# A two-layer decode step on one core: joint maximum before the second exponent, values in rows of (d, j), and the last wo in wide products

## The chip, the core and the metric

The kernel runs on one core of one Trainium2 chip. The time is device microseconds of one execution of the whole program, the median of several runs. The engines are TensorE (PE in the profile; PEld is its weight load), VectorE (DVE), ScalarE (ACT), GpSimd (POOL) and SyncE (SP), which here only issues transfers. SBUF is the on-chip memory of 128 partitions, PSUM the memory into which TensorE writes, in eight banks of 512 fp32 per partition.

## What is computed

Two attention layers and two feed-forward layers alternate, for a batch of 4 and one new token each, all in fp32. Both attention layers read the same caches and weights, both feed-forwards the same weights.

```python
def _A_ref(x, k_cache, v_cache, wq, wo):      # caches: (B=4, Hkv=8, Sk=4096, Dh=128); Hq = 32
    q = (x @ wq).reshape(B, Sq, Hq, Dh).transpose(0, 2, 1, 3)
    k, v = jnp.repeat(k_cache, 4, axis=1), jnp.repeat(v_cache, 4, axis=1)
    p = _softmax(jnp.einsum("bhqd,bhkd->bhqk", q, k) * Dh ** -0.5)
    o = jnp.einsum("bhqk,bhkd->bhqd", p, v)
    return o.transpose(0, 2, 1, 3).reshape(B, Sq, Hq * Dh) @ wo
def _B_ref(x, w1, w3, w2):                    # D = 512, F = 1792
    return (_silu(x @ w1) * (x @ w3)) @ w2
x = A_x
for _ in range(2):
    x = x + _A_ref(_layernorm(x), A_k_cache, A_v_cache, A_wq, A_wo)
    x = x + _B_ref(_layernorm(x), B_w1, B_w3, B_w2)
```

## The kernel before

**Data.** The host lays caches and weights out as one array of rows, 128 partitions wide, in the order in which they are used. SBUF holds one large buffer `space` of 218 slots of 1 KB per partition. The table LOADS lists the transfers in order: (first slot in the source, number of slots, place in `space`). `pump` issues the next transfer on SyncE's queue as soon as its place is free, and `done` frees a place behind the last product that reads it. Some rows stay in SBUF for the second layer, so 296.8 MB come from HBM in all.

**Attention.** A group is one key head with its four query heads. Layer 0 takes the groups 0 to 7, layer 1 the groups 7 to 0. The 4096 keys of a group come in two halves, `first` and `last`. TensorE, VectorE and ScalarE work in the order of the code; nothing reorders it:

- `score` multiplies q with eight tiles of keys into the bank `scores` (128 x 512: rows are batch, block of keys j and head; the columns are 512 keys). `between` puts other products behind a given tile: the turning of the group before (`turn_o`, tile 3), its wo product (`gather_o`, tile 5).
- `maximum` takes each row's negated maximum over its own half, `exponent` the exponential and its row sum, `turn` transposes p on TensorE and copies it out as pT, `weigh` multiplies pT with the values into the bank o_ps[0] or o_ps[1].
- `join_maxima` finds the maximum of each head over all its rows, by a 32 x 32 transpose on VectorE (`across`), and two factors that bring the rows of either half to it; `join_sums` joins the sums and takes the reciprocal.
- `finish` scales both banks into `both`, masks out the blocks that don't belong to the row, and adds the four blocks j up into `o`. The last group of a layer does it with one accumulation on VectorE for each block instead, so that those of o_ps[0] run beside the second `weigh`.
- q is made for two groups at a time: `share_q` leaves partial products in four bands of the bank `wide`, `take_q` evicts and scales them, `turn_q` adds the bands and transposes, `copy_q` places the result.
- wo: `gather_o` makes 4 wide products (8 x 512), whose four bands `take_o` evicts and `spread_o` adds up. The last group's `project_o` makes 16 products of 128 columns that need no such sum. A product in fp32 shows as two in the profile.

`busy` issues products of a unit matrix that nobody reads. `layernorm`, `feed_forward` and `down` follow, and in layer 0 `turn_over` leads to the next layer.

Of the kernel before, what the change touches and what calls it, by code (L numbers as in the profile page):

```python
# [8 lines left out]
F32 = mybir.dt.float32  # L9
# [6 lines left out]
REP = HQ // HKV  # L16
# [65 lines left out]
def tile_decode_layers(ctx: ExitStack, tc: tile.TileContext, rows, out):  # L82
# [116 lines left out]
    nc.vector.tensor_scalar(block, block, 2.0, None, op0=ALU.mult)  # L199
    nc.vector.tensor_copy(block[:, NB:], block[:, 0:NB])  # L200
# [37 lines left out]


# [99 lines left out]
    def spread_out():  # L339
        rows = across(rstd[:, 0:1])[:, 0:B]  # L340
        nc.vector.scalar_tensor_tensor(rows, rows, 1.0, alike, op0=ALU.mult, op1=ALU.mult, accum_out=spread)
# [43 lines left out]
    def exponent(i, ps, acc, scale=None):  # L385
        p = work.tile([P, NT, P], F32, name="p", bufs=1)
        nc.scalar.activation(p.rearrange("p n s -> p (n s)"), ps, AF.Exp, bias=acc[:, i:i + 1],  # L387
                             scale=1.0 if scale is None else scale, accum_out=acc[:, 2 + i:3 + i])
        return p
# [15 lines left out]
    def join_maxima(acc):  # L405
        nc.vector.tensor_tensor(acc[:, 6:7], acc[:, 0:1], acc[:, 1:2], op=ALU.min)
        rows = across(acc[:, 6:7])
        rows3 = rows.rearrange("p (j r) -> p j r", r=REP)
        nc.vector.tensor_tensor(rows3, rows3, other.unsqueeze(1).to_broadcast([P, 2 * NB, REP]), op=ALU.add)
        nc.vector.tensor_reduce(acc[:, 7:8], rows, axis=AX.X, op=ALU.min)  # L410
        nc.scalar.activation(acc[:, 4:6], acc[:, 0:2], AF.Exp, bias=acc[:, 7:8], scale=-1.0)

    def join_sums(acc, at_end):
        nc.vector.tensor_tensor(acc[:, 8:10], acc[:, 2:4], acc[:, 4:6], op=ALU.mult)
        nc.vector.tensor_tensor(acc[:, 10:11], acc[:, 8:9], acc[:, 9:10], op=ALU.add)
        rows = across(acc[:, 10:11])
        rows3 = rows.rearrange("p (j r) -> p j r", r=REP)
        nc.vector.scalar_tensor_tensor(rows3, rows3, 1.0, alike.unsqueeze(1).to_broadcast([P, 2 * NB, REP]),
                                       op0=ALU.mult, op1=ALU.mult, accum_out=acc[:, 11:12])
        nc.vector.reciprocal(acc[:, 11:12], acc[:, 11:12])  # L420
        if at_end:
            nc.vector.scalar_tensor_tensor(acc[:, 16:24].rearrange("p (i j) -> p i j", i=2),
                                           block.rearrange("p (i j) -> p i j", i=2), acc[:, 11:12],
                                           acc[:, 4:6].unsqueeze(2).to_broadcast([P, 2, NB]),
                                           op0=ALU.mult, op1=ALU.mult)
        else:
            nc.vector.tensor_scalar(acc[:, 16:16 + NB], block[:, 0:NB], acc[:, 11:12], None, op0=ALU.mult)
# [19 lines left out]
    def finish(layer, g, c, p, acc, at_end):  # L447
# [3 lines left out]
        join_sums(acc, at_end)  # L451
        if not at_end:
            both = work.tile([P, NB * DH], F32, name="both", tag="p", bufs=1)
            nc.scalar.activation(both, o_ps[0], AF.Copy, scale=acc[:, 4:5])  # L454
            weigh(layer, g, c, 1, pT)
            nc.vector.scalar_tensor_tensor(both, o_ps[1], acc[:, 5:6], both, op0=ALU.mult, op1=ALU.add)  # L456
            blocks = both.rearrange("p (j d) -> p j d", j=NB)
            nc.vector.tensor_tensor(blocks, blocks, acc[:, 16:16 + NB].unsqueeze(2).to_broadcast([P, NB, DH]), op=ALU.mult)  # L458
            o = work.tile([P, DH], F32, name="o", tag="pT", bufs=1)
            nc.vector.tensor_reduce(o, both.rearrange("p (j d) -> p d j", j=NB), axis=AX.X, op=ALU.add)  # L460
            return o
        o = work.tile([P, DH], F32, name="o", tag="p", bufs=1)
        nc.vector.tensor_scalar(o, o_ps[0][:, 0:DH], acc[:, 16:17], None, op0=ALU.mult)

        def add(s, js):
            for j in js:
                nc.vector.scalar_tensor_tensor(o, o_ps[s][:, j * DH:(j + 1) * DH],  # L467
# [17 lines left out]
    def project_o(layer, g):  # L485
        w = wo_of(g)
        for h in range(REP):
            for k in range(KC):
# [3 lines left out]
        nc.vector.scalar_tensor_tensor(x_sb, x_ps, 1.0, x_sb, op0=ALU.mult, op1=ALU.add,  # L492
                                       accum_out=rowsum)
# [125 lines left out]
    for layer in range(LAYERS):  # L619
# [5 lines left out]
        else:  # L625
# [5 lines left out]
            turn_q(take_q(spread), len(gs))  # L631
# [4 lines left out]
        for n, (g, (first, last)) in enumerate(order):  # L636
# [12 lines left out]
            pT = turn(p, nc.scalar.copy)  # L649
            between = {}  # L650
            if n in shared:
                shares = take_q(spread if len(gs) > 1 else rstd[:, 0:1])
# [12 lines left out]
            if layer and n == 0:  # L665
                spread_out()
# [11 lines left out]
        busy(BUSY[1])  # L678
        project_o(layer, g)
        busy(BUSY[2])  # L680
# [51 lines left out]
```

## Time and profile before

| | |
|---|---|
| median of 3 runs | 705.98 us (704.12 to 706.36) |
| the profiled execution | 702.22 us, its span 700.4 us |
| busy: PE, PEld, DVE, ACT, POOL | 408.4, 125.7, 128.1, 58.6, 3.4 us |
| moved | 297.35 MB, 425 GB/s on the mean |
| mean granted TensorE clock | 0.803 of full speed |
| chain of waits | DMA 68%, PE 26%, DVE 2% of the span |

The profile's page is of one execution. "Busy" is time in which an engine works on an instruction; the slices cut the span into 40 equal parts of 17.5 us. In a group's line stand the code's line, the engine, the operation, output and input by the program's names, their shapes, the count, the busy time with the mean of one in ns, and the idle time before them with what ended it. In a timeline a row is the start, the length, the engine and the instructions merged in it, in brackets the idle time of the engine ahead.

### The profile page before, as it was taken

To read this page: it belongs to the slowest core of one execution; us is meant where nothing else is said; L and a number is where in the kernel's file an instruction comes from. 1 tells how busy PE (TensorE), PEld (TensorE's weight loads), DVE (VectorE), ACT (ScalarE), POOL (GpSimd) and SP (SyncE) were. 2 spreads that over 40 slices of the span, in tenths; PEclk is the share of its full clock that TensorE was granted. 3 is DMA by queue.
4 is the path that set the end of the run, shared out by engine and by line. 5 is a ranking of instruction groups with operands and counts; after the bars stand their busy time and mean duration, and the time that the engine had idled before them with its cause. 6 is when DMAs were issued, how large, how long until landed. Compare 5 with 4: busy or idle time off the path is not lost.

```text
span 700.4 us, 7226 instructions
## 1 busy us (share of the span) xinstructions
PE 408.4 (58%) x3164; PEld 125.7 (18%) x3164; DVE 128.1 (18%) x394; ACT 58.6 (8%) x136; POOL 3.4 (0%) x15
## 2 busy tenths in 40 slices
PE   1245576545664519667686895544554626655677
PEld 0011121111211103121233331111111101111123
DVE  3012002120110103221221332011101201111322
ACT  0010000100100001010111300000100101001100
POOL 0000000000000000000000000000000000000000
PEclk9677668766788669877799998677968958688989
DMA  9999999999999999999999999999999999999997
GB/s 408 434 416 423 454 438 417 430 438 443 419 421 442 437 424 424 432 429 434 414 420 373 423 433 440 447 427 418 436 443 426 439 418 448 430 428 419 429 420 286
DMA packets 12704, 297.35 MB, mean 425 GB/s; under 512 B 1408, under 2 KB 1536, under 8 KB 4480
## 3 DMA queue, kind: packets, MB, share of 16 engines
q1 hardware_dynamic: 12672, 296.88, 99.1%
q8 instruction: 25, 0.41, 0.2%
q14 instruction: 7, 0.06, 0.0%
HBM read 296.81 MB, written 0.07 MB: 424 GB/s over the span
## 4 chain that ended last, share of the span: by engine, by line
DMA 68%; PE 26%; DVE 2%; another core or an unknown queue 1%; issue 1%; ACT 0%; SPq 0%; DVEq 0%; ACTq 0%
DMA space<-in_rows 68%; PE o L436 15%; PE scores L369 6%; PE turned L394 1%; PE o L525 1%; PE sums_ps L350 1%; DVE pT L396 1%; PE stored L290 1%; PE stored L571 0%; DVE o L467 0%; PE sums_ps L334 0%; PE sums_ps L489 0%; SPq L153 0%; PE sums_ps L579 0%
## 5 line engine op out<-in xcount | busy, mean ns | idle before, releaser
L369 PE MATMUL scores<-space,qT 128*32 128x512 f32 x1024 | 167.2, 737 | 135.0 <-DMA space<-in_rows 134.3
L436 PE MATMUL o<-space,pT 128*16 128x512 f32 x1024 | 148.4, 705 | 106.0 <-DMA space<-in_rows 97.5
L369 PEld LDWEIGHTS scores<-space,qT 128*32 128x32 f32 x1024 | 36.3, 126 | 215.3 <-issue 180.0
L436 PEld LDWEIGHTS o<-space,pT 128*16 128x16 f32 x1024 | 32.7, 108 | 202.7 <-issue 160.4
L381 DVE TENSOR_REDUCE acc<-scores 128x1 f32<-128x512 f32 x32 | 22.1, 691 | 183.7 <-PE scores L369 183.7
L387 ACT ACTIVATE p<-scores,acc 128x512 f32<-128x512 f32 x30 | 20.6, 687 | 412.9 <-DVE acc L381 305.1
L394 PE MATMUL turned<-ident,p 128*128 128x128 f32 x128 | 23.3, 310 | 16.6 <-ACT p L387 16.6
L396 DVE COPY pT<-turned 128x256 f32<-128x256 f32 x16 | 6.8, 424 | 141.2 <-PE turned L394 141.2
L394 PEld LDWEIGHTS turned<-ident,p 128*128 128x128 f32 x128 | 14.9, 152 | 49.2 <-ACT p L387 31.7
L456 DVE SCALAR_TENSOR_TENSOR both<-o,acc,both 128x512 f32<-128x512 f32 x14 | 10.5, 750 | 56.5 <-PE o L436 56.5
L454 ACT ACTIVATE both<-o,acc 128x512 f32<-128x512 f32 x14 | 9.6, 687 | 119.0 <-PE turned L394 119.0
L479 DVE COPY oT<-sums_ps 128x16 f32<-128x16 f32 x16 | 2.8, 175 | 86.2 <-PE sums_ps L478 86.2
L334 PE MATMUL sums_ps<-space,xT 128*32 128x512 f32 x120 | 16.7, 680 | 2.8 <-DMA space<-in_rows 2.8
L525 PE MATMUL o<-space,xT 128*32 128x192 f32 (+1 forms) x256 | 13.9, 355 | 3.8 <-DMA space<-in_rows 1.9
L460 DVE TENSOR_REDUCE o<-both 128x128 f32<-128x512 f32 x14 | 14.4, 1028 | 0.5
L499 PE MATMUL stored<-space,oT 128*8 128x512 f32 x104 | 13.6, 595 | 0.0
L478 PE MATMUL sums_ps<-columns,o 128*128 128x16 f32 x32 | 7.6, 315 | 5.4 <-DVE o L460 4.1
L478 PEld LDWEIGHTS sums_ps<-columns,o 128*128 128x128 f32 x32 | 6.0, 234 | 25.7 <-issue 13.3
L350 PEld LDWEIGHTS sums_ps<-same,shares 128*128 128x128 f32 x64 | 8.6, 209 | 10.1 <-DVE shares L345 5.1
L248 PE MATMUL o<-columns,same 128*32 128x1 f32 x64 | 2.0, 181 | 14.5 <-DVE columns L626 13.5
L350 PE MATMUL sums_ps<-same,shares 128*128 128x8 f32 (+1 forms) x64 | 9.3, 272 | 0.9 <-DVE shares L345 0.9
L458 DVE TENSOR_TENSOR both<-both,acc 128x512 f32<-128x512 f32 x14 | 9.7, 692 | 0.5
(119 smaller groups left out, 166.1 us busy)
## 6 DMA issues: line engine op xcount, KB each, us to landing
space<-in_rows SPq DMA_DIRECT2D x7, 4096.0 KB, 24.8
space<-in_rows SPq DMA_DIRECT2D x3, 6144.0 KB, 31.9
space<-in_rows SPq DMA_DIRECT2D x8, 2048.0 KB, 25.7
space<-in_rows SPq DMA_DIRECT2D x2, 7168.0 KB, 43.1
space<-in_rows SPq DMA_DIRECT2D x4, 3072.0 KB, 26.4
space<-in_rows SPq DMA_DIRECT2D x11, 1024.0 KB, 13.1
space<-in_rows SPq DMA_DIRECT2D x3, 3584.0 KB, 17.1
space<-in_rows SPq DMA_DIRECT2D x2, 5120.0 KB, 22.8
```

The lines of the kernel that those rows point to most:

```text
L334: nc.tensor.matmul(wide[32 * k:32 * k + 32, :], window(k, j), w[:, k, :], start=(j == 0), stop=(j == len(gs) - 1))
L350: nc.tensor.matmul(misc[:, h * n * B:(h + 1) * n * B], shares[:, h * DH:(h + 1) * DH], same[:, 0:n * B], start=True, stop=True)
L369: nc.tensor.matmul(ps[32 * b:32 * b + 32, :], qT[:, at:at + 32], u, start=(m < 2), stop=(m >= TILES - 2))
L381: nc.vector.tensor_reduce(acc[:, i:i + 1], ps, axis=AX.X, op=ALU.max, negate=True)
L387: nc.scalar.activation(p.rearrange("p n s -> p (n s)"), ps, AF.Exp, bias=acc[:, i:i + 1], scale=1.0 if scale is None else scale, accum_out ...
L394: nc.tensor.transpose(pt[:, n, :], p[:, n, :], ident)
L396: copy(pT, pt.rearrange("p n (b r) -> p n b r", b=B)[:, :, :, 0:ROW])
L436: nc.tensor.matmul(o_ps[i][32 * b:32 * b + ROW, :], pT[:, r // 2, b, :], t[:, j * NB * DH:(j + 1) * NB * DH], start=(r < 2), stop=(r >= TI ...
L460: nc.vector.tensor_reduce(o, both.rearrange("p (j d) -> p d j", j=NB), axis=AX.X, op=ALU.add)
L478: nc.tensor.matmul(at, o, head, start=True, stop=True)
L499: nc.tensor.matmul(bank[32 * h:32 * h + WIDE, :], oT[:, h, :], w[:, h, :], start=first, stop=last)
L525: nc.tensor.matmul(bank[32 * j:32 * j + 32, s], window(k), w[:, j], start=(k == 0), stop=(k == KC - 1))
```

## The change

1. `join_maxima` runs ahead of a group's second exponent, which then uses the joint maximum (acc column 7). The second half needs no factor of its own; the first half's stands in column 4. A few small instructions of `join_maxima`, `join_sums` and the setup go, and one (`mine`) comes in the last group.
2. The values' rows are laid out on the host as (d, j) instead of (j, d). The four blocks of a column then lie side by side; the last group's accumulations read every fourth element of PSUM.
3. ScalarE instead of VectorE evicts q (`take_q`), and VectorE instead of ScalarE copies the first pT and scales the first half into `both`. The scale of q is folded into `spread`, which layer 1 now makes ahead of its first exponent.
4. `unit` issues two unit products of 512 columns into o_ps[0] in layer 0's group 6, between the first scores and the turning of the first p.
5. In layer 1 the last group's wo goes through `gather_o`, `take_o` and `spread_o`, and the `busy` products around it are left out. Layer 0 keeps `project_o`.
6. In LOADS two transfers of 16 slots become one of 32.

```diff
-    (992, 32, 154), (1024, 32, 186), (1056, 16, 0), (1072, 16, 96), (1088, 16, 112), (1104, 8, 128), (1112, 8, 136),
+    (992, 32, 154), (1024, 32, 186), (1056, 16, 0), (1072, 32, 96), (1104, 8, 128), (1112, 8, 136),
...
+    def unit(bank):
+        nc.tensor.matmul(bank.rearrange("p (k c) -> p k c", k=KC), ident, ident.unsqueeze(1).to_broadcast([P, KC, P]),
+                         start=True, stop=True)
...
-    def take_q(factor):
+    def take_q():
         shares = work.tile([P, REP * DH], F32, name="shares", tag="p", bufs=1)
-        nc.vector.tensor_scalar(shares, wide, factor, -D * SCALE, op0=ALU.mult, op1=ALU.mult)
+        nc.scalar.activation(shares, wide, AF.Copy, scale=spread)
...
-        nc.scalar.activation(acc[:, 4:6], acc[:, 0:2], AF.Exp, bias=acc[:, 7:8], scale=-1.0)
...
         if not at_end:
             both = work.tile([P, NB * DH], F32, name="both", tag="p", bufs=1)
-            nc.scalar.activation(both, o_ps[0], AF.Copy, scale=acc[:, 4:5])
+            nc.vector.tensor_scalar(both, o_ps[0], acc[:, 4:5], None, op0=ALU.mult)
             weigh(layer, g, c, 1, pT)
-            nc.vector.scalar_tensor_tensor(both, o_ps[1], acc[:, 5:6], both, op0=ALU.mult, op1=ALU.add)
-            blocks = both.rearrange("p (j d) -> p j d", j=NB)
-            nc.vector.tensor_tensor(blocks, blocks, acc[:, 16:16 + NB].unsqueeze(2).to_broadcast([P, NB, DH]), op=ALU.mult)
-            o = work.tile([P, DH], F32, name="o", tag="pT", bufs=1)
-            nc.vector.tensor_reduce(o, both.rearrange("p (j d) -> p d j", j=NB), axis=AX.X, op=ALU.add)
+            nc.vector.tensor_tensor(both, both, o_ps[1], op=ALU.add)
+            blocks = both.rearrange("p (d j) -> p d j", j=NB)
+            nc.vector.tensor_tensor(blocks, blocks, mine.unsqueeze(1).to_broadcast([P, DH, NB]), op=ALU.mult)
+            o = both[:, 0:DH]
+            nc.vector.tensor_reduce(o, blocks, axis=AX.X, op=ALU.add)
             return o
...
-        nc.vector.tensor_scalar(o, o_ps[0][:, 0:DH], acc[:, 16:17], None, op0=ALU.mult)
+        split = [bank.rearrange("p (d j) -> p j d", j=NB) for bank in o_ps]
+        nc.vector.tensor_scalar(o, split[0][:, 0], acc[:, 16:17], None, op0=ALU.mult)
...
             maximum(0, ps, acc, scale)
+            if scale is not None:
+                spread_out()
             if n in shared:
...
-            p = exponent(0, ps, acc, scale)
+            elif layer == 0 and n == TURN - 1:
+                unit(o_ps[0])
+                unit(o_ps[0])
+            p = exponent(0, 0, ps, acc, scale)
...
-            pT = turn(p, nc.scalar.copy)
+            pT = turn(p, nc.vector.tensor_copy)
...
             maximum(1, ps, acc, scale)
-            p = exponent(1, ps, acc, scale)
+            join_maxima(acc)
+            p = exponent(1, 7, ps, acc, scale)
+            nc.scalar.activation(acc[:, 4:5], acc[:, 0:1], AF.Exp, bias=acc[:, 7:8], scale=-1.0)
             if n + 1 < len(order):
                 copy_q(gs, order[n + 1][0])
-            join_maxima(acc)
             weigh(layer, g, first, 0, pT)
...
-        busy(BUSY[1])
-        project_o(layer, g)
-        busy(BUSY[2])
+        if layer:
+            gather_o(layer, g, wide)
+            spread_o(take_o(wide), True)
+        else:
+            busy(BUSY[1])
+            project_o(layer, g)
+            busy(BUSY[2])
+        nc.vector.scalar_tensor_tensor(x_sb, x_ps, 1.0, x_sb, op0=ALU.mult, op1=ALU.add, accum_out=rowsum)
```

How the instructions stand on two engines at the places that matter. TensorE behind layer 1's last `weigh`, before (L243 is `busy`, L478 `turn_o`, L489 `project_o`, L248 the mean, L530 the old x, L525 w1):

```order
L436 MATMUL o_102<-space,pT 16x512 x16
L243 MATMUL scores<-ident 128x512
L478 MATMUL sums_ps<-columns,o 128x16
L243 MATMUL scores<-ident 128x128
L489 MATMUL sums_ps<-space,oT 8x128 x16
L243 MATMUL scores<-ident 128x256
L248 MATMUL o_102<-columns,same 32x1 x4
```

and now (L245 is `busy`, L477 `turn_o`, L496 `gather_o`, L506 `spread_o`, L250 the mean):

```order
L434 MATMUL o_100<-space,pT 16x512 x16
L245 MATMUL scores<-ident 128x512
L477 MATMUL sums_ps<-columns,o 128x16
L496 MATMUL sums_ps<-space,oT 8x512 x4
L506 MATMUL sums_ps<-shares,same 8x128 x4
L250 MATMUL o_100<-columns,same 32x1 x4
```

Sixteen narrow products have become four wide ones and four that add their bands up, with VectorE's eviction of the bands between the two; two `busy` products are gone. VectorE from the first maximum of layer 0's second group to its joined sums, before (L381 `maximum`, L345 `take_q`, L325 `copy_q`, L406 to L410 `join_maxima`, L396 the copy of pT, L414 and L415 the sums):

```order
L381 TENSOR_REDUCE acc<-scores 128x1
L345 TENSOR_SCALAR shares<-sums_ps,columns 128x512
L381 TENSOR_REDUCE acc<-scores 128x1
L325 COPY qT<-sums_ps 128x8x4
L406 TENSOR_TENSOR acc<-acc 128x1
L402 STREAM_TRANSPOSE rows<-acc 128x32
L409 TENSOR_TENSOR rows<-rows,columns 128x32
L410 TENSOR_REDUCE acc<-rows 128x1
L396 COPY pT<-turned 128x256
L414 TENSOR_TENSOR acc<-acc 128x2
L415 TENSOR_TENSOR acc<-acc 128x1
```

and now (L383 `maximum`, L398 the copies of pT, L408 to L412 `join_maxima`, L327 `copy_q`, L415 the sums):

```order
L383 TENSOR_REDUCE acc<-scores 128x1
L398 COPY pT<-turned 128x256
L383 TENSOR_REDUCE acc<-scores 128x1
L408 TENSOR_TENSOR acc<-acc 128x1
L404 STREAM_TRANSPOSE rows<-acc 128x32
L411 TENSOR_TENSOR rows<-rows,columns 128x32
L412 TENSOR_REDUCE acc<-rows 128x1
L327 COPY qT<-sums_ps 128x8x4
L398 COPY pT<-turned 128x256
L415 SCALAR_TENSOR_TENSOR acc<-acc 128x1
```

The eviction of q has left VectorE and the first copy of pT has come to it; the joint maximum stands ahead of the copy of q, and the second exponent on ScalarE waits for it.

More of the change, by code (lines that the diff above doesn't have):

```diff
@@ L383, in maximum, with exponent @@
             nc.vector.tensor_tensor(acc[:, i:i + 1], acc[:, i:i + 1], scale, op=ALU.mult)
[L385 removed]
+    def exponent(i, at, ps, acc, scale=None):
         p = work.tile([P, NT, P], F32, name="p", bufs=1)
[L387 removed]
+        nc.scalar.activation(p.rearrange("p n s -> p (n s)"), ps, AF.Exp, bias=acc[:, at:at + 1],
                              scale=1.0 if scale is None else scale, accum_out=acc[:, 2 + i:3 + i])
@@ L630, in tile_decode_layers @@
             share_q(layer, gs)
-            turn_q(take_q(spread), len(gs))
+            turn_q(take_q(), len(gs))
             copy_q(gs, order[0][0])
@@ L648, in tile_decode_layers @@
                 pump()
-            pT = turn(p, nc.scalar.copy)
+            pT = turn(p, nc.vector.tensor_copy)
             between = {}
             if n in shared:
-                shares = take_q(spread if len(gs) > 1 else rstd[:, 0:1])
+                shares = take_q()
                 between[2] = lambda shares=shares, n=len(gs): turn_q(shares, n)
```

29 lines of the change are left out of this document (10 added, 19 removed).

## The prediction

> **What bounds the kernel now.** I read the page's slices first, then the queues, then the chain of waits, and last the end of the run in short stretches. The slices and the queue row say how the span is filled:
>
> ```profile
> DMA  9999999999999999999999999999999999999997
> GB/s 408 434 416 423 454 438 417 430 438 443 419 421 442 437 424 424 432 429 434 414 420 373 423 433 440 447 427 418 436 443 426 439 418 448 430 428 419 429 420 286
> ...
> q1 hardware_dynamic: 12672, 296.88, 99.1%
> ```
>
> One queue moves 296.88 MB, and its packets fill 99.1% of sixteen engines' span. TensorE's 58% is no bound. An instruction made shorter can shorten the run in two ways only: it closes a hole in this stream, or it lies behind the stream's end. The thinnest place of the stream, at the change of layers (slice 22, 373 GB/s), and the end, in short stretches:
>
> ```profile
> 371.00:372.00 1.00, 0.81 (x14) 0.29 (x16) 0.52 (x2) 0.98 (x1) 0.00 (x0) 1.00 0.79 270
> 692.00:694.00 2.00, 1.72 (x13) 0.56 (x9) 0.52 (x2) 0.00 (x0) 0.00 (x0) 1.00 1.01 392
> 694.00:696.00 2.00, 2.00 (x21) 0.34 (x23) 0.41 (x3) 0.00 (x0) 0.00 (x0) 1.00 0.51 189
> 696.00:698.00 2.00, 1.44 (x44) 0.75 (x40) 0.93 (x2) 0.00 (x0) 0.00 (x0) 1.00 0.10 35
> ```
>
> The last two columns are the DMA share and GB/s. The only hole worth naming is a fifth of 1 us at 371; at the end the stream is full to 694 and runs dry by about 697. The chain of waits, from its last transfer on:
>
> ```profile
> 649.82 18.76 DMA space<-in_rows
> ...
> 668.71 6.37 PE o L436 x32
> ...
> 681.11 0.36 DVE o L467
> ...
> 681.51 0.40 PE sums_ps L478 x2
> ...
> 682.23 1.01 PE sums_ps L489 x32
> ...
> 685.48 2.67 PE o L525 x56
> ...
> 694.21 1.88 PE stored L571 x16
> ...
> 696.11 0.70 DVE shares L504
> ...
> 696.85 0.41 PE sums_ps L509 x8
> 697.26 0.48 PE sums_ps L579 x16
> ...
> 697.76 0.29 DVE space L684
> ```
>
> From 668.71 on, no transfer stands in it: 29 us of products, accumulations and the feed-forward, one behind the other. So two things end together, the stream (dry by 697) and this chain (last products 697.26 to 697.74). Whatever lengthens the chain lengthens the run; whatever shortens it gains nearly nothing, since the last w2 rows land in the same microsecond.
>
> **The last wo, wide.** The narrow form and its successor stand in the timeline of the tail; the wide form is there for another group:
>
> ```profile
> 654.37 1.04 PE L499 MATMUL stored<-space,oT 128*8 128x512 f32 x8
> ...
> 682.18 1.06 PE L489 MATMUL sums_ps<-space,oT 128*8 128x128 f32 x32
> ...
> 683.30 0.29 DVE L492 SCALAR_TENSOR_TENSOR space<-sums_ps,space 128x128 f32<-128x128 f32 x1 [1.18 <-PE sums_ps L489]
> ```
>
> Narrow: 32 products, 1.06 us, then VectorE adds them to x at 683.30. Wide: 8 products, 1.04 us. But their sum lies in four bands of wide and has to come out by take_o (0.70, the row at 696.11) and spread_o (0.41, the row at 696.85), before the same addition. VectorE started 0.06 after the products here, and the products 0.04 after VectorE at 696.85. So -0.02 + 0.06 + 0.70 + 0.04 + 0.41 = +1.19 us, all of it on the chain, with no cover: behind it wait the mean, x's turning and every product of w1. The two fill-in products taken out with it ran beside VectorE's copy and addition: gain 0 to 0.05, I take 0.
>
> **Values in rows of (d, j).** Groups by line:
>
> ```profile
> L460 DVE TENSOR_REDUCE o<-both 128x128 f32<-128x512 f32 x14 | 14.4, 1028 | 0.5
> ...
> L479 DVE COPY oT<-sums_ps 128x16 f32<-128x16 f32 x16 | 2.8, 175 | 86.2 <-PE sums_ps L478 86.2
> L325 DVE COPY qT<-sums_ps 128x32 f32<-128x32 f32 x15 | 2.7, 181 | 1.2 <-PE sums_ps L350 1.2
> L192 DVE TENSOR_REDUCE columns<-ident 128x16 f32<-128x128 f32 x1 | 0.4, 369 | 0.0
> L626 DVE TENSOR_REDUCE columns<-space 128x1 f32<-128x128 f32 x1 | 0.3, 285 | 7.5 <-DMA space<-in_rows 7.5
> ```
>
> L460 reads with a step of 128 elements and takes 1028 ns where 512 elements in a row take 0.70 (the row at 696.11). In the new order its four inputs lie side by side: about -0.33 in each of 14 groups. The price comes back in each layer's last group: its seven accumulations and the first now read PSUM with a step of four elements. Four stand on the chain (the last is the row at 681.11). Bounds: SBUF read at such a step cost 369 against 285 ns for 128 elements (L192, L626), +0.084 each, so +0.34 for four; PSUM read at that step (L479, 16 elements, 175 ns) costs what its length leads one to expect beside L325 (32 elements, 181 ns), so 0. L479 reads the same memory at the same step: I take 0 and keep +0.34. [...]
>
> **The 14 shorter groups.** Where this 0.33 goes is in the list of waits (us in total, times, longest):
>
> ```profile
> PEld sums_ps L478 <- DVE o L460: 9.6, 6, 1.9
> ```
>
> TensorE waits for o in 6 groups, so it may gain 6 x 0.33 = 2.0 us of its own time. These groups lie where the stream is full: buffers come free a little sooner and the transfers queue a little longer. On the end: 0; if the cover were gone, -2.0 us.
>
> **Joint maximum ahead of the second exponent.** It adds a wait: ScalarE stands until VectorE's minimum over the heads is done, behind it only the small exponent and the next group; TensorE's second turning waits for that exponent. One group in time:
>
> ```profile
> 306.70 3.60 PE L436 MATMUL o<-space,pT 128*16 128x512 f32 x32
> ...
> 307.74 0.69 ACT L387 ACTIVATE p<-scores,acc 128x512 f32<-128x512 f32 x1 [6.79 <-DVE qT L325]
> ...
> 308.33 0.19 ACT L387 ACTIVATION_READ_ACCUMULATOR p<-scores,acc 128x1 f32 x1
> 308.35 0.19 DVE L410 TENSOR_REDUCE acc<-rows 128x1 f32<-128x32 f32 x1
> ...
> 310.24 0.65 PE L394 MATMUL turned<-ident,p 128*128 128x128 f32 x4
> ```
>
> The exponent ended at 308.52; now it starts where L410 ended (308.54, less 0.18 for the copy of q that goes behind it) and needs 307.74 to 308.52, 0.78, again: about 309.2, against 310.24 when TensorE comes for it, having weighed the first half. Hidden with 1.0 us to spare; without that cover it would cost the 0.6 by which it starts later in each group. What the joint maximum saves (one instruction of the sums, two columns of a small exponent) stands beside the second weighing: 0.
>
> **ScalarE evicts q, VectorE turns the first p.** The two 128x512 and 128x256 evictions behind the first exponent change engines, and the scaling of the first half goes to VectorE, inside the second weighing (3.60 us for such a half, against 0.70 for 512 columns on VectorE). Cost 0; without the cover the difference of two evictions, under 0.1 us, or that 0.70 in each group. In layer 1's first group q comes behind two copies back from PSUM on ScalarE; its use is two tiles of scores later. The spread of rstd, moved ahead of the first exponent there, stands behind the maximum, beside that exponent: 0. Two setup instructions less, before the second load has landed: 0.
>
> **Unit products in group 6.** They fill TensorE's wait for the first exponent:
>
> ```profile
> 299.42 1.12 PE L394 MATMUL turned<-ident,p 128*128 128x128 f32 x4 [1.96 <-ACT p L387]
> 300.47 4.48 PE L369 MATMUL scores<-space,qT 128*32 128x512 f32 x18
> ...
> 679.81 1.12 PE L243 MATMUL scores<-ident 128*128 128x512 f32 x2
> ```
>
> One such product takes 1.12 us at full clock, two at half clock near 4, in a wait of 1.96: up to +2 for TensorE, or up to -2.2 if they bring the full clock earlier, as the scores behind it took 4.48 at half of it. What the freed buffers then take is one transfer:
>
> ```profile
> space<-in_rows SPq DMA_DIRECT2D x1, 4096.0 KB, 14.3
> ```
>
> It was issued at the end of this weighing and landed 14.3 us later, though 4.19 MB need 9.9 at 425 GB/s: some 4 us of stream stood ahead of it. On the end: 0 in both directions.
>
> **Two loads become one.** 4.19 MB in the slice with 414 GB/s instead of the mean 425 took 10.1 instead of 9.9: between 0 and -0.26, I take -0.1. The joint load waits for the later of two buffers, issued over 20 us before its turn.
>
> **Sum.** +1.19 - 0.1 = +1.1 us; up to 0.1 of it may still fall to the stream's own end, so +1.0. Against the profiled execution (span 700.4, run 702.22) that is 701.4 and 703.2. The median of the three runs, 705.98, lies 3.76 above it; I carry that over: **707.0**, +0.14%. About 0.3% (2.1 us) is what a measurement of this kernel can tell from no change.
>
> **Rivals.**
> *The end hides it.* If the stream, not the chain, ends last in most runs (they are 3.76 us longer than the profiled one, perhaps by slower transfers), the +1.19 vanishes: 705.9. Against it: the last products follow each other without a gap behind L504 and L509. 0.15.
> *Slower: the clock falls in the last feed-forward.* TensorE now idles twice more, 0.8 us each, from the last accumulation to the first product of w1. The granted clock changes in steps of 3.41 us in this trace, and such steps show the limit, by TensorE's busy time (second pair) and the granted clock of the next one:
>
> ```profile
> 121.33:124.74 3.41, 1.59 (x16) 0.44 (x8) 0.69 (x1) 0.88 (x3) 0.00 (x0) 1.00 1.07 461
> 124.75:128.15 3.40, 2.28 (x12) 0.68 (x16) 0.00 (x0) 0.26 (x1) 0.00 (x0) 0.50 1.04 448
> 493.38:496.79 3.41, 1.40 (x16) 0.42 (x16) 0.00 (x0) 0.78 (x2) 0.00 (x0) 1.00 1.05 452
> 496.80:500.20 3.40, 3.40 (x29) 1.34 (x21) 0.75 (x1) 0.37 (x1) 0.00 (x0) 1.00 0.93 405
> ```
>
> 1.59 us busy was once too little, 1.40 once enough. The new tail has the pieces 0.40, 1.04 and 0.41 from 681.51 to 684.44, then the mean; its emptiest 3.41 us hold about 1.75 of them, so the clock should hold. With the strided +0.34 ahead, 1.45, and it may fall. Then the 64 products of w1 (2.67 us for 56 of them, so 3.1) take twice as long: 707.0 + 0.34 + 3.1 = 710.4. [...] 0.10.
> *Slower: the stream starves.* Near 371 the next free buffer decides; if a chain step there came 1 to 2 us later (strided reads in layer 0's last group), the hole of 0.2 us grows by as much: 708 to 709. Against it: nothing was added to layer 0's chain but 0 to 0.34. 0.07.
> *Faster: the earlier frees count.* If the 2.0 us of TensorE's waits were worth as much to the stream, 707.0 - 2.0 = 705.0, and with the 2.2 of group 6, 702.8. It needs holes in the stream that slices and queue row don't show. 0.10.
>
> **Numbers.** Forecast 0.58 (with the pieces' bounds, +0.8 to +1.5 us). Range 704.6 to 709.4: it takes in the hidden end, the starved stream and the milder of the two faster sums, with a microsecond for the runs' own spread (704.12 to 706.36), and leaves out the fallen clock and the quicker sum. Slower by over 0.3% (above 708.1): 0.10 for the clock, 0.05 of the starved stream, 0.06 of the forecast by the runs' spread, 0.21. Faster (below 703.9): 0.05 of the faster case and 0.03 of spread, 0.08. Within: 0.71.
>
> **What would show it.** take_o and spread_o between the last wo and the mean, some 1.2 us, and all behind them later by that; the last transfer's landing where it was; the reduction to o near 0.7; the last accumulations at 0.36 or 0.44; granted clock 1.0 from 674 to the end. I am wrong if the stream's mean rate or its holes differ, or if the tail starts elsewhere.

## The result, and the profile after

| | before | changed |
|---|---|---|
| median | 704.73 us (702.60 to 706.50) | 708.26 us (704.31 to 714.27) |
| runs | 19 | 19 |
| profiled execution, its span | 702.22, 700.4 us | 710.53, 708.5 us |

The ratio is 1.0054 [1.0035, 1.0074]: 3.8 us slower, where +1.0 was forecast. 708.26 lies inside the predicted range, but the difference is beyond the 0.3% below which no change can be told from this kernel's own spread. Single disturbed runs, of 752 and 928 us in two experiments below, are left out of the ratios but not of the medians given there, which without them are 705.68 us for 706.12 and 705.04 for 705.08. The page of the changed kernel, the lines that answer to those of before:

```profile
span 708.5 us, 7145 instructions
...
DMA  9999999999999999999999999999999999999994
GB/s 418 414 415 466 415 422 446 432 426 437 419 435 450 416 433 423 433 433 419 426 369 346 413 432 442 445 433 412 455 430 422 438 429 434 429 438 414 424 421 180
...
q1 hardware_dynamic: 12528, 296.88, 98.1%
```

The same bytes fill a smaller share of a longer span. Three slices stand out: numbers 21 and 22, at the change of layers, have 369 and 346 GB/s for 420 and 373, and the last 180 for 286. In stretches of 10 us, first before, then the changed kernel (the last three columns are granted clock, DMA share, GB/s):

```profile
355.00:365.00 10.00, 7.78 (x100) 3.73 (x100) 2.83 (x12) 0.78 (x3) 0.55 (x1) 1.00 0.99 421
365.00:375.00 10.00, 7.20 (x114) 4.11 (x118) 1.90 (x5) 2.38 (x4) 0.00 (x0) 1.00 0.98 375
375.00:385.00 10.00, 6.96 (x155) 3.83 (x143) 1.15 (x6) 0.37 (x2) 0.00 (x0) 0.83 1.00 374
385.00:395.00 10.00, 8.57 (x84) 3.24 (x88) 2.62 (x9) 3.91 (x10) 0.70 (x1) 1.00 1.03 421
```

```profile
355.00:365.00 10.00, 8.42 (x72) 2.77 (x72) 4.56 (x17) 2.87 (x6) 0.00 (x0) 0.79 0.98 418
365.00:375.00 10.00, 8.84 (x134) 4.65 (x138) 2.48 (x10) 1.18 (x3) 0.55 (x1) 1.00 0.79 288
375.00:385.00 10.00, 6.66 (x125) 3.81 (x117) 1.07 (x6) 1.20 (x2) 0.00 (x0) 0.74 0.95 345
385.00:395.00 10.00, 7.10 (x121) 2.79 (x113) 2.91 (x13) 3.12 (x10) 0.70 (x1) 0.92 1.02 381
```

A fifth of the stream is missing between 365 and 375, and GB/s stay low behind it. Outside this place both streams run alike: 150 MB had landed at 350.4 to 350.6 us in every trace. From 155 to 170 MB it took 37.8 us before and 41.6 now: the stream is 3.8 us late from there on, and nothing gives that back.

Not all of these 3.8 us are the change's doing: the profiled execution of before was a quick one at this place. The other profiles, with the experiments below, tell how much. Without the joint load the same 15 MB took 37.8 to 38.9 us in three profiles in which TensorE's clock was low for 3.4 us between 355 and 400, and 39.3 to 40.8 us in four in which it was low for 10.2 to 13.7. With the joint load they took 39.7 us (clock low for 4.1), and 41.6 twice (11.1 here and 13.7). At a like clock the joint load thus goes with some 1.4 us, and a clock that was low for 7 to 10 us longer with some 2 us, which met kernels without the joint load as well. That the low clock is the cause of these 2 us was not tested by itself.

Why it stalls stands in the timeline of TensorE in layer 0's last group (start, length, operation, and in brackets what ended the idle time ahead), before:

```profile
345.40 2.47 PE L436 MATMUL o<-space,pT 128*16 128x512 f32 x16 [2.44 <-DMA space<-in_rows]
...
350.39 4.25 PE L436 MATMUL o<-space,pT 128*16 128x512 f32 x24 [1.47 <-DVE acc L420]
...
361.84 0.64 PE L525 MATMUL o<-space,xT 128*32 128x256 f32 x8 [0.81 <-DVE xT L264]
```

and of the changed kernel:

```profile
350.50 3.61 PE L434 MATMUL o<-space,pT 128*16 128x512 f32 x16 [7.60 <-DMA space<-in_rows]
...
355.68 5.36 PE L434 MATMUL o<-space,pT 128*16 128x512 f32 x32 [0.52 <-DVE pT L398]
...
366.57 0.64 PE L522 MATMUL o<-space,xT 128*32 128x256 f32 x8 [0.81 <-DVE xT L266]
```

The second half of a first weighing starts 5.1 us later, since TensorE stands 7.60 us for a load. The joint load (1072, 32) carries the values of this half and also the head of the next ones, and nobody may read the first part before the whole has landed: at 350.46, as late as the second of the two loads of before (350.26), where the first of them had landed at 345.36. Behind the stop the products run in part at half clock (5.36 us for 32, where 3.63 are needed at the full one), the first product of w1 starts 4.7 us later, and the buffers come free later by as much. SP, which issues the loads, shows it; its longest wait at this place, before and now:

```profile
SPq L153 <- ACT o L223: 15.6, 1, 15.6
```

```profile
SPq L153 <- ACT o L221: 20.3, 1, 20.3
```

At the other end of the run, the timeline of the tail:

```profile
685.24 0.40 PE L477 MATMUL sums_ps<-columns,o 128*128 128x16 f32 x2 [0.58 <-DVE o L466]
...
685.90 1.04 PE L496 MATMUL sums_ps<-space,oT 128*8 128x512 f32 x8 [0.27 <-DVE oT L478]
687.01 0.69 DVE L501 TENSOR_SCALAR shares<-sums_ps 128x512 f32<-128x512 f32 x1 [1.17 <-PE sums_ps L496]
...
687.76 0.40 PE L506 MATMUL sums_ps<-shares,same 128*8 128x128 f32 x8 [0.81 <-DVE shares L501]
688.23 0.29 DVE L686 SCALAR_TENSOR_TENSOR space<-sums_ps,space 128x128 f32<-128x128 f32 x1 [0.53 <-PE sums_ps L506]
...
689.59 0.64 PE L522 MATMUL o<-space,xT 128*32 128x256 f32 x8 [0.34 <-DVE xT L266]
...
690.11 6.19 PE L522 MATMUL o<-space,xT 128*32 128x256 f32 x88
```

and its windows, cut at the steps of the clock:

```profile
686.92:690.33 3.41, 1.83 (x43) 1.05 (x43) 1.78 (x7) 0.00 (x0) 0.00 (x0) 1.00 0.98 414
690.33:693.74 3.41, 3.41 (x41) 1.96 (x37) 0.16 (x1) 0.00 (x0) 0.55 (x1) 0.50 0.99 411
...
697.00:699.00 2.00, 1.78 (x34) 1.04 (x34) 0.18 (x2) 0.00 (x0) 0.00 (x0) 1.00 0.62 234
699.00:701.00 2.00, 1.94 (x15) 0.56 (x17) 0.71 (x5) 0.00 (x0) 0.00 (x0) 1.00 0.18 67
701.00:703.00 2.00, 1.84 (x32) 0.65 (x24) 0.56 (x2) 0.00 (x0) 0.00 (x0) 1.00 0.00 0
```

The stream is dry by about 700, and products go on to 704: the chain now ends last, alone. The two profiled executions lie 8.1 us of span apart, more than their medians. These 8.1 are made up of four parts: turn_o (L477) starts 3.7 us later because of the stream; from the weighing's end to the first product of w1 it takes 5.99 us for 4.92 (+1.1); w1 and w3 take 8.82 us for 7.25 (+1.6), since the clock fell at 690.33 for one step; and the last store, issued at 704.45 for 698.08, ends 1.7 us later behind its issue than before. That is most likely chance: it took 4.1 us in this execution, 2.4 to 2.6 in the wide experiments below, and 4.2 in the kernel before without fill-in products, which has neither the wide wo nor the joint load.

### The profile page after: what moved, and what is told of

Same layout as the page of the kernel before. It is cut to its first block, busy times and chain, and to the rows that moved or that the text cites. A ratio compares the mean times of both kernels' runs of the same rounds, so it can differ in the third digit from the quotient of the medians.

```text
span 708.5 us, 7145 instructions
## 1 busy us (share of the span) xinstructions
PE 418.3 (59%) x3148; PEld 126.9 (18%) x3148; DVE 132.0 (19%) x401; ACT 46.8 (7%) x114; POOL 3.4 (0%) x15
## 5 line engine op out<-in xcount | busy, mean ns | idle before, releaser
L371 PE MATMUL scores<-space,qT 128*32 128x512 f32 x1024 | 164.8, 726 | 130.3 <-DMA space<-in_rows 129.6
L434 PE MATMUL o<-space,pT 128*16 128x512 f32 x1024 | 154.4, 727 | 108.5 <-DMA space<-in_rows 101.8
L383 DVE TENSOR_REDUCE acc<-scores 128x1 f32<-128x512 f32 x32 | 22.1, 691 | 172.1 <-PE scores L371 172.1
L398 DVE COPY pT<-turned 128x256 f32<-128x256 f32 x32 | 13.6, 424 | 180.6 <-PE turned L396 180.6
L396 PE MATMUL turned<-ident,p 128*128 128x128 f32 x128 | 22.9, 306 | 15.1 <-ACT p L389 15.1
L396 PEld LDWEIGHTS turned<-ident,p 128*128 128x128 f32 x128 | 14.9, 152 | 49.4 <-ACT p L389 28.6
L336 PE MATMUL sums_ps<-space,xT 128*32 128x512 f32 x120 | 19.3, 770 | 3.5 <-DMA space<-in_rows 3.5
L454 DVE TENSOR_TENSOR both<-both,o 128x512 f32<-128x512 f32 x14 | 9.6, 688 | 52.5 <-PE o L434 52.5
L478 DVE COPY oT<-sums_ps 128x16 f32<-128x16 f32 x16 | 2.8, 174 | 88.4 <-PE sums_ps L477 88.4
L496 PE MATMUL stored<-space,oT 128*8 128x512 f32 x104 | 13.5, 593 | 0.0
L250 PE MATMUL o<-columns,same 128*32 128x1 f32 x64 | 2.0, 181 | 14.9 <-DVE columns L623 13.6
L452 DVE TENSOR_SCALAR both<-o,acc 128x512 f32<-128x512 f32 x14 | 10.4, 745 | 0.0
L522 PEld LDWEIGHTS o<-space,xT 128*32 128x32 f32 x256 | 8.3, 119 | 7.8 <-issue 1.8
L458 DVE TENSOR_REDUCE both<-both 128x128 f32<-128x512 f32 x14 | 9.6, 686 | 0.5
L576 PE MATMUL sums_ps<-space,hT 128*4 128x128 f32 x144 | 7.0, 340 | 3.9 <-DMA space<-in_rows 3.9
```

The costliest lines, as they stand in the source:

```text
L336: nc.tensor.matmul(wide[32 * k:32 * k + 32, :], window(k, j), w[:, k, :], start=(j == 0), stop=(j == len(gs) - 1))
L371: nc.tensor.matmul(ps[32 * b:32 * b + 32, :], qT[:, at:at + 32], u, start=(m < 2), stop=(m >= TILES - 2))
L383: nc.vector.tensor_reduce(acc[:, i:i + 1], ps, axis=AX.X, op=ALU.max, negate=True)
L396: nc.tensor.transpose(pt[:, n, :], p[:, n, :], ident)
L398: copy(pT, pt.rearrange("p n (b r) -> p n b r", b=B)[:, :, :, 0:ROW])
L434: nc.tensor.matmul(o_ps[i][32 * b:32 * b + ROW, :], pT[:, r // 2, b, :], t[:, j * NB * DH:(j + 1) * NB * DH], start=(r < 2), stop=(r >= TI ...
```

## The experiments

Two accounts stood against each other. By the first the joint load starves the stream at the change of layers, and this makes most of the loss. By the second the wide wo does, by its length and by a clock that falls in the feed-forward behind it. The ratios are against executions of the kernel before that ran beside each experiment.

**The changed kernel with the two loads apart.**

```diff
-    (992, 32, 154), (1024, 32, 186), (1056, 16, 0), (1072, 32, 96), (1104, 8, 128), (1112, 8, 136),
+    (992, 32, 154), (1024, 32, 186), (1056, 16, 0), (1072, 16, 96), (1088, 16, 112), (1104, 8, 128), (1112, 8, 136),
```

> The changed kernel with the joint load of 32 slots split again into two of 16. Theory L (the joint load lands as a whole, so layer 0's last group gets the second half of its first values some 5 us later, all behind it is late, and the feed-forward's loads go out too late to keep the stream full): the weighing that waited until 350.5 us in the changed kernel starts near 345.4 again, the first w3 load goes out near 359.4 instead of 364.1, and the time falls by 2.5 to 3.5 us against the changed kernel, leaving +0.5 to +1.5 against the kernel before. Theory T (all of the loss lies behind the last weighing: wide wo and a fallen clock): no change against the changed kernel, still +3 to +4 against before.

Measured: 707.83 us in 7 runs, ratio 1.0061 [1.0036, 1.0086]. The loss stays, so the joint load isn't its larger part: the first account's +0.5 to +1.5 is missed, and the second's +3 to +4 is what came (+4.3). In the trace the first account's stop did go: that weighing starts at 345.60 again, and the load behind it is issued at 359.6 instead of 364.1; the time didn't fall with it. The clock of the tail, in windows cut at its steps:

```profile
682.76:686.17 3.41, 1.84 (x18) 0.53 (x18) 1.23 (x5) 0.00 (x0) 0.00 (x0) 1.00 1.00 423
686.17:689.58 3.41, 3.26 (x40) 1.81 (x44) 1.00 (x7) 0.00 (x0) 0.55 (x1) 0.50 0.99 413
689.58:693.00 3.42, 3.42 (x44) 1.96 (x40) 0.00 (x0) 0.00 (x0) 0.00 (x0) 0.50 1.00 407
```

It is halved for two steps, and w1 with w3 takes 9.91 us for 7.25.

**The changed kernel with the narrow wo and its fill-in products.**

```diff
-        if layer:
-            gather_o(layer, g, wide)
-            spread_o(take_o(wide), True)
-        else:
-            busy(BUSY[1])
-            project_o(layer, g)
-            busy(BUSY[2])
+        busy(BUSY[1])
+        project_o(layer, g)
+        busy(BUSY[2])
```

> The changed kernel with the narrow wo and its fill-in products back in layer 1, the joint load kept. Theory L: 1 to 2 us are won (1.2 for the eviction and the sum over the bands, up to 1.5 for a clock that fell in some runs), +2 to +3 against before remain. Theory T: all of the loss goes, within 0.5 us of before.

Measured: 704.94 us, 1.0022 [1.0005, 1.0040]. By the ratios more than half of the loss goes with the wide form; the +1.5 us that stay are below the first account's +2 to +3 and above the second's 0.5. The joint load is still in it.

**Both edits together.**

> The changed kernel with both undone: two loads of 16 slots, narrow wo with its fill-in products. Both theories: within 0.7 us of before, either way; if something else in the change costs or gains, it shows here. Theory L and T differ only in which of the two edits brings it back.

Measured: 704.44 us, 0.9999 [0.9983, 1.0014]. All the rest of the change (joint maximum, rows of (d, j), exchanged evictions, unit products) sums to nothing, within 1.2 us either way.

**The kernel before with the joint load alone.** The edit is the first one, turned round.

> The kernel before with nothing changed but the two loads of 16 slots made one of 32. Theory L: +2.5 to +3.5 us, with the second half of that weighing starting near 350.5 instead of 345.4 us and the stream's share under 0.9 for some us behind 364. Theory T, and the recorded sum: 0 to -0.3 us.

Measured: 705.54 us, 1.0021 [1.0005, 1.0036], +1.5 us: neither the 0 to -0.3 of the recorded sum nor the 2.5 to 3.5 of the first account. Its timeline repeats the changed kernel's:

```profile
350.49 3.62 PE L436 MATMUL o<-space,pT 128*16 128x512 f32 x16 [7.78 <-DMA space<-in_rows]
...
355.50 3.63 PE L436 MATMUL o<-space,pT 128*16 128x512 f32 x32 [0.58 <-DVE pT L396]
...
364.65 0.64 PE L525 MATMUL o<-space,xT 128*32 128x256 f32 x8 [0.81 <-DVE xT L264]
```

The stop is the same; the products behind it kept the full clock here, and w1 starts 2.8 us later than before instead of 4.7.

**The kernel before with the wide wo alone**, without fill-in products in layer 1 (the diff of the change, part 5).

> The kernel before with the wide wo alone (and without its fill-in products). Theory C: +2.5 to +3.5 us, with a lower granted clock in the last feed-forward in a good part of the runs and a wider spread of times. The recorded sum: +1.2.

Measured: 706.75 us, 1.0037 [1.0019, 1.0055], +2.6 us. Here too the clock is halved behind it; w1 and w3 take 9.92 us.

**The wide wo with fill-in products**, loads apart:

```diff
         if layer:
+            busy(1)
             gather_o(layer, g, wide)
+            busy(2)
             spread_o(take_o(wide), True)
+            busy(1)
```

> The wide wo with the clock held: the changed kernel with split loads, and unit products of 128, 256 and 128 columns in TensorE's waits of that tail (behind the turning of o, beside the eviction of the bands, behind the sum over them). Theory C (the wide wo costs 1.2 us by its length, and the rest because the emptier tail lets the clock fall ahead of w1): full clock to the end, +1.0 to +1.5 against before, some 2 us less than with split loads alone. Theory W (the wide form itself costs 3 us, by its products or what they wait for): +3 as with split loads alone, whatever the clock.

Measured: 705.58 us, 1.0019 [1.0004, 1.0034]; the loss without the fill-in products was +4.3 us, and +1.3 are left. The timeline of its tail:

```profile
685.95 1.04 PE L496 MATMUL sums_ps<-space,oT 128*8 128x512 f32 x8
686.93 0.70 PE L245 MATMUL scores<-ident 128*128 128x256 f32 x2
687.81 0.41 PE L506 MATMUL sums_ps<-shares,same 128*8 128x128 f32 x8 [0.18 <-DVE shares L501]
...
690.15 4.51 PE L522 MATMUL o<-space,xT 128*32 128x256 f32 x88
```

The 88 products of w1 and w3 in the last row take 4.51 us, as in the kernel before; in the changed kernel the same 88 took 6.19. The way from the weighing to w1 is as long as in the other wide forms (5.98 us for 4.92), the time lost is 1.3 us (0.3 to 2.4 by the interval): this is the length of the wide form by itself. What it costs beyond that in the other kernels is the clock.

**The kernel before without the two fill-in products of layer 1.**

```diff
-        busy(BUSY[1])
+        busy(0 if layer else BUSY[1])
         project_o(layer, g)
-        busy(BUSY[2])
+        busy(0 if layer else BUSY[2])
```

> The kernel before with the two fill-in products around layer 1's narrow wo left out. Theory C in its first form (the emptiness comes from the eviction and the sum, not from the missing fill-in): the tail's emptiest 3.41 us stay above 55% busy, no change, within 0.5 us. If the clock falls in the last feed-forward here too and the time grows by 1 to 3 us, the missing fill-in products are the cause by themselves.

Measured: 706.12 us, 1.0022 [1.0004, 1.0040], a miss: slower where no difference was expected. The clock held behind its wo in the profiled execution (703.98 us), in which the way to w1 was 0.1 us shorter and gained nothing:

```profile
695.93 0.62 PE L579 MATMUL sums_ps<-space,hT 128*4 128x128 f32 x16 [0.20 <-DMA space<-in_rows]
```

The last products waited for the last load, as the prediction said of a shorter chain. That the other runs lost their time to the clock is likely from the shares worked out in the last section (0.33 in its emptiest 3.41 us, where the clock fell behind steps of up to 0.39), but none of them was profiled.

**Another joint load in the kernel before.**

```diff
-    ... (1072, 16, 96), (1088, 16, 112), (1104, 8, 128), (1112, 8, 136),
+    ... (1072, 16, 96), (1088, 24, 112), (1112, 8, 136),
```

> A control for the joint load: the kernel before with another pair made one, the 16 slots from 1088 and the 8 from 1104, so that there are as many loads as in the changed kernel but none holds both the rest of group 7's first values and the head of its last ones. Theory L (a joint load lands as a whole and its first reader waits for it): the first weighing starts again near 345.4 us and the time stays within 0.5 us of before. If the number or size of loads mattered: +1 to +1.5 as with the joint load of the change.

Measured: 705.08 us, 1.0014 [1.0000, 1.0028]. It was to be a control without the wait, and isn't one:

```profile
345.51 3.61 PE L436 MATMUL o<-space,pT 128*16 128x512 f32 x16 [2.88 <-DMA space<-in_rows]
...
352.93 6.29 PE L436 MATMUL o<-space,pT 128*16 128x512 f32 x32 [2.76 <-DMA space<-in_rows]
...
364.74 0.64 PE L525 MATMUL o<-space,xT 128*32 128x256 f32 x8 [0.81 <-DVE xT L264]
```

The first weighing starts where it did; now the second waits, for the head of its values, which this load holds back. w1 starts 2.9 us late. Its timeline shows the same with another load: the first reader of the joint load waits for all of it, 2.76 us in the row at 352.93. Its time alone would also fit the rival, a cost of fewer and larger loads as such (+1 to +1.5); no run here excludes that such a cost exists beside the wait.

**The unit products taken out** (both edits of the third experiment, and `unit` away).

```diff
-            elif layer == 0 and n == TURN - 1:
-                unit(o_ps[0])
-                unit(o_ps[0])
```

> The changed kernel with loads split, wo narrow, and the two unit products of group 6 left out: what is left is the joint maximum, the rows of (d, j) and the evictions. As recorded, the unit products are worth nothing to the end: within 0.5 us of before and of the same kernel with them. If they bring the clock up early enough to matter, it is 0.5 to 1.5 us slower than with them.

Measured: 704.42 us, 0.9995 [0.9982, 1.0007], against 0.9999 [0.9983, 1.0014] with them: no worth shows.

**Products that hold the clock at the change of layers.** The clock falls there in every profile without such products, at a place that differs between runs. `hum` multiplies the unit matrix as `busy` does, and nobody reads the result. The edit adds fourteen such products of 128 columns (the expectations below say twelve), three in layer 0's w3 and eleven in its w2, here in the kernel before:

```diff
+                if layer == 0 and m < 5:
+                    hum(2, 1)
...
+                if layer == 0 and 5 < m < 12:
+                    hum(0, 1)
...
-            part(up, "w3b", (1, 2, 3))
+            for k in (1, 2, 3):
+                part(up, "w3b", (k,))
+                hum(2, 1)
```

> The kernel before with twelve more fill-in products of 128 columns between the last w3 rows and the w2 rows of layer 0, where TensorE waits for transfers. Theory H (the stream takes the same time in all runs outside 355 to 400 us, and what differs there is whether the clock falls beside the w2 rows and is still low when layer 1's first group should free its buffers): the clock stays full from 365 to 400 in every run, the median falls by 0.8 to 1.5 us to the lower of the two clusters of times of the kernel before (702.4 to 703.6). Rival (the two clusters come from the transfers themselves, or the added products are in the way of the rows they wait for): no change, or up to 1 us slower.

Measured: 704.73 us (703.61 to 706.03) against 704.95 (702.59 to 707.39), 0.9996 [0.9986, 1.0005]. The same in the third experiment's kernel:

> The same fill-in products in the changed kernel with its loads split and its wo narrow again. Theory H: the same gain, 0.8 to 1.5 us under before; if the remaining parts of the change (rows of (d, j), joint maximum, evictions) help layer 1's first group free its buffers sooner, up to 0.5 more. Rival: no change against before.

Measured: 704.26 us (703.33 to 705.07), 0.9989 [0.9979, 0.9999]. Between 355 and 400 the clock stays at 1.00 in both, and the spread halves, but the lowest times go as well: loads are issued up to 1.8 us later in the first and 2.2 in the second than in the profile of before, since the added products lie in front of those that free buffers. So only five of them, one in w3 and four in w2:

```diff
+                if layer == 0 and m == 2:
+                    hum(2, 1)
...
+                if layer == 0 and m in (7, 9, 11):
+                    hum(0, 1)
...
-            part(up, "w3b", (1, 2, 3))
+            part(up, "w3b", (1, 2))
+            hum(2, 1)
+            part(up, "w3b", (3,))
```

> The changed kernel with loads split, wo narrow, and five fill-in products instead of twelve beside layer 0's w3 and w2 rows. With twelve the clock held, but the products stood ahead of rows that had landed, and buffers came free up to 1.8 us later. Theory H2 (holding the clock and freeing early both count): the clock holds in most runs, loads go out as early as in the kernel before, and the median falls 1.0 to 1.8 us under before. Rival (the stream's holes there come from elsewhere): within 0.7 us of before, like the kernel with twelve.

Measured: 703.25 us (702.47 to 705.88) against 704.67, 0.9991 [0.9973, 1.0009]. Its windows:

```profile
375.00:385.00 10.00, 7.31 (x159) 4.36 (x149) 1.23 (x6) 0.37 (x2) 0.00 (x0) 1.00 0.99 366
385.00:395.00 10.00, 8.68 (x88) 3.32 (x92) 2.52 (x11) 4.23 (x10) 0.70 (x1) 1.00 1.02 419
```

No step at half clock, and the stream as full as before. It has the lowest median of all kernels run, but its interval holds 1. Only the interval of the kernel with fourteen products ends short of 1, at 0.9999, with 0.8 us of gain; as one of a dozen experiments, and under the 0.3% that can be told here, that doesn't show a version that beats the kernel before.

## Why the prediction was right or wrong

**Luck: the time.** The forecast of 707.0 us misses 708.26 by only 1.3, because it was carried over from a median of three runs, 705.98, and nineteen runs gave 704.73. Counted from there, the same sum gives 705.7 and the same range 703.4 to 708.2, which 708.26 just leaves. The difference, 3.8 us for 1.0, is the honest measure. What came was the case "slower by over 0.3%", with its chance of 0.21, by both of its rivals at once: the stream at about its price, the clock below its price. The prediction had them only one at a time. Its own signs of being wrong came too: the stream's holes differ, and the tail starts 3.7 us later in the profiled execution.

**Right: what bounds the kernel before.** Stream and chain end together, and a shorter chain gained nothing in the one profile of it (the kernel without fill-in products), a longer one cost its length.

**Right: the wide wo's +1.19 on the chain.** Its pieces were 1.04, 0.69 and 0.40 in the trace, the way from the weighing to w1 grew by 1.06 to 1.11 in the wide forms, and with the clock held it cost 1.3 us (0.3 to 2.4).

**Right: everything that was put at 0.** Together it is 0 (0.9999 [0.9983, 1.0014]); single terms under a microsecond could still cancel each other. Two groups of the changed kernel answer to those shown of before:

```profile
L458 DVE TENSOR_REDUCE both<-both 128x128 f32<-128x512 f32 x14 | 9.6, 686 | 0.5
...
L466 DVE SCALAR_TENSOR_TENSOR o<-o,acc,o 128x128 f32<-128x128 f32 x14 | 4.9, 350 | 4.5 <-PE o L434 4.1
```

The reduction is at 686 ns for 1028, and the accumulations over every fourth element of PSUM take 350 ns, as the row at 681.11 did. So L479 was the right neighbour, and the +0.34 kept for the range didn't come.

**Wrong: two loads become one, "between 0 and -0.26, I take -0.1".** It measured +1.5 alone ([+0.4, +2.5] by its interval). I looked at when the load is issued, "over 20 us before its turn", and at the queue's rate, and not at who reads it. Its first reader already waited for the first half, and now waits for the second as well, of which it needs nothing. The timeline of before had the place in it, in the row at 345.40: half a weighing that waited 2.44 us for the first of the two loads. The gain was also too large: by the median a packet of 32768 bytes took 1215 ns and one of 16384 took 613, so a pair saves 11 ns, and with 128 pairs on sixteen engines the merge saves at most 0.09 us.

**Wrong in size: the starved stream, 0.07, "if a chain step there came 1 to 2 us later" the hole "grows by as much".** This mechanism came, by another cause than the strided reads: the step came 2.8 to 4.7 us later, and the stream stood idle for longer at the change of layers: counted as idle share of the sixteen engines from 355 to 400 us, for 3.2, 2.4 and 1.9 us in the three profiles with this joint load (the changed kernel, the one before with the load, the one with the narrow wo), for 2.3 with the other joint load, and for 0.8 to 1.7 us in seven without a joint load and without products that hold the clock there. The means of the three and of the seven, 2.5 and 1.2, are some 1.2 apart, near the 1.5 by which the load alone lengthened the runs.

**Wrong in chance: the fallen clock, 0.10.** The price was near: 3.1 us was said, 1.6 (one step) to 2.7 (two steps) was measured. It was no rare case but came in all three profiles of a wide wo without fill-in products. The step that failed is "its emptiest 3.41 us hold about 1.75 of them, so the clock should hold": the rows it stood on ordered windows by the length of TensorE's rows, and this measure doesn't decide. 1.84 us in the window at 682.76 above were too few, 1.40 had once been enough. I should have seen that the two rows of before already contradicted each other: 1.59 fell and 1.40 held. With it failed the term of the two fill-in products, "gain 0 to 0.05, I take 0": taken out of the kernel before they cost 1.5 us (0.3 to 2.8), and put back beside the wide wo they won 3 (+4.3 became +1.3).

The sum by the runs: wide wo +2.6 (of it 1.3 for its length, the rest clock), joint load +1.5, all else 0: +4.1, where +3.8 [+2.5, +5.2] was measured. What stays open: taking the joint load out of the changed kernel gained nothing that shows (1.0061 against 1.0054, intervals of some 0.25% each side), while adding it to the kernel before cost 0.2%. With these intervals the two agree, but whether the two losses simply add up isn't shown.

## What to carry to other kernels

Before two loads are joined, ask who reads the first bytes of the joint one and whether this reader waits already: its wait grows by the landing time of all the rest (here from 2.44 to 7.60 us). A product that does nothing but keep the clock belongs to the step of 3.41 us it covers (two of them taken out cost 1.5 us here, three put beside the wide wo won 3), so that whoever takes such products out, or makes an idle gap beside them, prices the clock for every phase at which its steps may fall. Where a kernel is bound by a stream with no holes, look for what makes the first hole rather than for what makes instructions shorter.

## What the hardware showed that was not expected

The clock changes in steps of 3.41 us: the 62 stretches of one granted clock in the trace of before begin whole steps apart, to 3 ns, and so do the 70 of the changed kernel. What sorts these steps is how much of a step the columns of products stream, not how long TensorE's rows are. Two products of 512 columns take 1.12 us and two of 128 take 0.47 (both L245), so 0.85 ns for a column and some 0.25 us beside them; in the weighing of before at 646.13 the next four products of 512 columns, which overlap, start every 0.43 us, 0.84 ns for a column, and in the one at 53.13, at half clock, every 0.85 us. Counting 0.84 ns for each column at full clock, twice that at half, and overlapping products once, the 409 steps of these two traces sort nearly without overlap: the clock fell behind steps with a share of up to 0.39 and stayed from 0.37 on; it rose from 0.73 on and stayed low up to 0.77. Of the two steps that the prediction shows, the one at 121.33, 1.59 us by rows, has a share of 0.35, and the clock fell; the one at 493.38, 1.40 us, has 0.41, and it held. The tail of before has 0.50 in its emptiest 3.41 us, wherever the step begins, more than any step behind which the clock fell in these two traces; the wide one without fill-in products has 0.30, with them about 0.5; the kernel before without fill-in products 0.33. The step ahead of each of the three falls in the tail had 0.33 to 0.34. TensorE did not stand idle through the step ahead of a fall: the window at 686.92 had 1.83 us of products, and the clock was halved behind it.

The phase of these steps differs from execution to execution (whole steps back from its boundaries, the first lies 1.86 us behind the start of the span in the trace of before, 0.83 in the changed kernel's, 0.1 in that of the changed kernel with the loads apart), and with it, by the shares above, whether a marginal step falls: the tail of the kernel before without fill-in products, 0.33 at its emptiest, kept the full clock in its profile. That fits the kernel's own spread, 702.59 to 707.39 beside the experiments with these products, which the products that held the clock at the change of layers brought down to 703.33 to 705.07 and 703.61 to 706.03. That the phase makes the whole of it isn't shown.
